# Attention, then two feed-forward layers, in one kernel on one core: a new plan for the first stage, a new weight conversion, and an addition by TensorE

## The chip, the cores and the metric

The kernel runs on one core of one Trainium2 chip. The metric is device time in microseconds (us) of one execution. The core has TensorE (matmul), VectorE, ScalarE, GpSimd and SyncE, which each run their own list of instructions in order and wait for one another by semaphores. SyncE issues nearly all DMA transfers.

## The reference

Three parts, in fp32 with inputs of the types that `setup_inputs()` gives:

- Attention over 4 batches, 8 heads, 576 positions, head size 64. Queries, keys and values are averaged over groups of 4 positions, full softmax attention runs on the 144 averages, and its output is repeated 4 times. To this is added a local attention in which a position sees only positions less than 4 away. So `x = out_up + out_local`, 2304 tokens by 512.
- First layer: `h = x @ w_in` (2048 columns), `g = s * relu(h)**2 + b`, `x = g @ w_out`.
- Second layer: `a = x @ w_a`, `c = x @ w_b` (1536 columns each), `out = (a * c) @ w_out`.

## The kernel before, in words

The matrices of the layers are multiplied with fp32 operands split in two parts, a high part in the faster fp32r type and the remainder as low part. Each product is three matmuls: high by high, high by low, low by high.

**Phase A** is the first layer. The tokens come in 6 blocks of 384. For each block, 16 steps f run over 128 columns of `w_in` each: four groups of three matmuls into the bank h (L1162 to L1164), ReLU (L1179) and square (L1183) on ScalarE, a copy that makes the high part (L1186, ScalarE), a subtraction for the low part (L1190, VectorE), and twelve matmuls into four banks acc (L1205 to L1207). **Phase B** is the second layer (L1269 on).

Before a block's products can start, its tokens must be there as high and low parts (xs). Blocks 0 and 1 get theirs from the **ramp**: six tiles of 128 tokens (`tile_job`, L802), which do the local attention on TensorE: scores (L843, L851), softmax on VectorE and ScalarE (L878 to L929), transposes (L937), products with the values (L956). VectorE adds the pooled output (L973) from upT, ScalarE makes the high part (L569), VectorE the low part (L573). Blocks 2 to 5 get theirs from 13 **band units** (`unit`, L988), which do the local attention on VectorE, some 17 us each; they start when the ramp has ended (L1664). For each batch, `down` (L630) does the pooled attention head pair by head pair: pooling of q and k (L654 on VectorE, L656 and L657 on GpSimd), scores (L688), softmax, transposes (L739), products with the pooled values (L760). For batches 1 to 3 the pooled values pv are made by transfers alone (`pool_in`, L611): a load by SyncE (L621) and three accumulating transfers by GpSimd for each half (L623), six in all, into one buffer.

**Weights** arrive as 64-bit floats, 512 KB a slice. A slice of phase A (32 of them, two for each f) is converted by `w_words` (L393) and `w_slice` (L439): ScalarE scales the high word into z (L414) and takes the low bits (L421), VectorE puts the sign in (L426) and joins both (L434), ScalarE copies the high part (L450), VectorE subtracts for the low part (L455).

**Order.** A planner in the kernel's Python code (`Program.order`, L168) simulates all engines with a fixed cost for each task and issues the task that can start first, ties by due time. Its list is the order of each engine's instructions on the chip. Due times hang on T0 (the wanted start of block 0) and the DUE constants (L71 to L76). Fill matmuls on zeros (`keep_warm`, L327) are put ahead of a task where the plan sees TensorE waiting, until block 0 has begun.

Of the kernel before, what the change touches and what calls it, by code (L numbers as in the profile page):

```python
# [17 lines left out]
HP = H // 2  # L18
# [5 lines left out]
TQ = 64  # L24
# [55 lines left out]
RAMP_BUFS = {"dq": 2, "dk": 2, "qd": 4, "kd": 4, "tq": 1, "tk": 1, "tv": 1, "e": 1, "x": 1, "z": 2}  # L80
# [7 lines left out]

ISSUE, QUEUE, DMA_START, POOL_START, DMA_LAND, POOL_NEXT = 0.46, 8, 1.29, 2.15, 1.18, 0.8
# [3 lines left out]
class Task:  # L93
    __slots__ = (
        "eng", "dur", "fn", "deps", "succ", "acq", "picks", "rel", "due", "lead", "share", "num", "left", "ready", "start",
        "end", "fill", "seen", "dma", "order", "wait",
# [3 lines left out]
class Clock:  # L100


    TICK, COLUMNS = 3.41333, 1.4

    def __init__(self):
        self.done = {}

    def run(self, start, work, share, keep=True):
        t = start
        while work > 1e-9:  # L110
            k = int(t / self.TICK + 1e-6)
            rate = 1.0 if self.done.get(k - 1, 0.0) >= self.COLUMNS else 0.5
            d = min(work / rate, (k + 1) * self.TICK - t)
            if keep:
                self.done[k] = self.done.get(k, 0.0) + d * rate * share
            work -= d * rate
            t += d
        return t
# [20 lines left out]
class Program:  # L139
# [8 lines left out]
    def add(self, eng, dur, fn, reads=(), writes=(), acq=(), rel=(), due=1e9, after=(), lead=0.0, share=1.0, seen=None, dma=(), order=0, wait=0.0):  # L148
# [5 lines left out]
        t.lead, t.share = lead, share  # L154
# [13 lines left out]
    def order(self):  # L168
# [9 lines left out]
        clock, warming, wire = Clock(), True, Wire()  # L178
        landed, adding = [], 0.0
        at["SP"] = 0.75  # L180
        at["PE"] = clock.run(1.07, 0.17 * WARM, 1.0)
# [9 lines left out]
        while len(out) < len(self.tasks):  # L191
            best = None
            for e in ENGINES:
                for t in avail[e]:
# [3 lines left out]
                    if e == "SP" and len(landed) >= QUEUE:  # L198
                        s = max(s, landed[-QUEUE])
# [34 lines left out]
            if t.eng == "PE":  # L234
                g0 = at["PE"]
# [41 lines left out]
def dve(n):  # L277
    return n / 960 + 0.065

# [10 lines left out]
def moe_chain(ctx, tc, qT, kT, vd, tq, tk, tv, qu, ku, vu, w_a1, w_o1, w_a2, w_b2, w_o2, sb, ident_d, bmask_d, emask_d, out):  # L290
# [30 lines left out]

    def bank(tag, shape, name):
        return ps.tile(shape, F32, tag=tag, name=name, bufs=4 if tag == "acc" else 2)

    pw = []

    def keep_warm(count):  # L327

        for _ in range(count):
            nc.tensor.matmul(out=pw[0], lhsT=wz[:, :128], rhs=wz, start=True, stop=True)  # L330

    def load(dst_src, nbytes, reads=(), writes=(), acq=(), rel=(), due=1e9, after=(), rows=128, pieces=1, base=0):
        def fn(picks):
            dst, src = dst_src(picks)
            nc.sync.dma_start(out=dst, in_=src)
# [35 lines left out]
    add("CTL", 0.0, warm_fn, acq=[("acc",)], due=-1e6)  # L371
# [21 lines left out]
    def w_words(k, spool, z, first, name, acq=(), after=()):  # L393
# [36 lines left out]
        add("DVE", 0.53, s_fn, [("low", k)], [("sg", k)], wait=PATIENCE)  # L430
# [5 lines left out]
        add("DVE", 0.6, b_fn, [("z", k), ("sg", k)], [name], rel=[ld_pick(ld), "stg"], wait=PATIENCE)  # L436
        return tz

    def w_slice(k, ph, lo_eng, after=()):  # L439
# [6 lines left out]
        w_words(k, ("w",), z, (), ("t", k), [(ph + "z",)], after)  # L446

        def h_fn(picks):
            wt[k] = slot(picks[0], F32R)
            A_.activation(out=wt[k][:, 0], in_=st["z"], func=ACTF.Copy)  # L450

        add("ACT", 0.52, h_fn, [("t", k)], [("wh", k)], [("w",)], wait=PATIENCE)
# [26 lines left out]
    def w_out(p, t, after, due=1e9):  # L479
# [8 lines left out]
        if t == 0:  # L488
# [8 lines left out]
            def s_fn(picks):  # L497
                nc.sync.dma_start(out=wod[p], in_=st["z"])
# [60 lines left out]
    def split_x(st, t0, n, xkey, ph, due):  # L559

        done = 0
        last = None
        while done < n:
# [4 lines left out]
            def hi(picks, i=i, o=o, w=w, done=done):  # L568
                A_.activation(out=xs["a", i][0][:, :, o:o + w], in_=st["x"][:, :, done:done + w], func=ACTF.Copy)  # L569

            def lo(picks, i=i, o=o, w=w, done=done):
# [6 lines left out]
            th = add("ACT", act(HP * w), hi, [xkey, ("slot", ("a", i))], [("xsh", i)], due=due)  # L578
            last = add(
                "DVE", dve(HP * w), lo, [xkey], [("xs", i)], due=due, after=[th] + ([last] if last else []),  # L580
                rel=[ph + "x"] if done + w == n else (),
# [29 lines left out]
    def pool_in(b, after, due):  # L611
# [3 lines left out]
        for r in range(4):  # L615
            for kh in range(2):
                def fn(p, r=r, kh=kh):
                    if r == kh == 0:
                        pooled[b] = upp.tile([HK, 2, HP, 2 * D], F32, tag="pv", name="pv", bufs=1)
                    if r == 0:  # L620
                        nc.sync.dma_start(out=pooled[b][:, kh], in_=src[:, kh, :, r])  # L621
# [5 lines left out]
                    [t[kh]] if r else [t[0]] if kh else after, order=kh if r == 0 else 0, seen=0.1, dma=[wires(HK, HP, 512, 0, r > 0)],  # L627
                )

    def down(b, hp, ph, pool_eng, due=1e9):  # L630
# [53 lines left out]
        def s_fn(p):  # L684
# [9 lines left out]
            "PE", 0.7, s_fn, [("qd", key), ("kd", key)], [("sc", key)], [wide, wide, E_SLOT[ph]],  # L694
            [ph + "qd", ph + "kd"], lead=LEAD, share=0.5)
# [48 lines left out]
        tt = add("PE", 0.52, t_fn, [("a", key), "ident"], [("at", key)], [wide, wide], lead=LEAD, share=0.5625)  # L744
# [10 lines left out]
        def o_fn(p):  # L755
# [46 lines left out]
    def tile_job(i, due):  # L802
# [35 lines left out]
        def s_fn(p):  # L838
# [22 lines left out]
            after=[mm["dS", bl, hp] for hp in range(HP)], lead=LEAD, share=0.55,  # L861
# [71 lines left out]
        def t_fn(p):  # L933
# [7 lines left out]
            lead=LEAD, share=0.75,  # L941
# [8 lines left out]

        def o_fn(p):
            o = st["o"] = bank(p[0], [128, HP, TT], "o")
            for hp in range(HP):
                for g in range(NQ):
                    for h in range(2):
# [3 lines left out]
                            rhs=st["aT"][:, h, hp, g * TQ:g * TQ + TQ], start=True, stop=True,  # L959
# [4 lines left out]
            "PE", 1.1, o_fn, [("taT", i), ("tv", i), ("slot", ("a", blk))] + [("up", b) for b in batches], [("to", i)], [WIDE],  # L964
            [pick(ts, 2), pick(t_v, 0)], lead=LEAD, share=0.8,
# [12 lines left out]

# [816 lines left out]
```

## Time and profile before

| | |
|---|---|
| median of 3 runs | 928.06 us (927.93, 928.06, 933.91) |
| profiled execution | 933.64 us, span 931.8 us |
| TensorE matmul busy | 909.6 us, 98% |
| VectorE busy | 781.5 us, 84% |
| ScalarE busy | 480.9 us, 52% |
| GpSimd busy | 72.4 us, 8% |

Times in the profile are us from the first instruction; the span ends with the last. A busy TensorE is not TensorE at its peak, since matmuls overlap in the records: a matmul of 384 columns shows 0.34 us and the next one starts 0.18 us later. In slices of 1/40 of the span, TensorE's granted clock is full but for the third (0.9) and the fourth (0.7).

### The profile page before, as it was taken

What the parts mean: (1) busy time and instruction counts of PE and PEld (TensorE: products, weight loads), DVE (VectorE), ACT (ScalarE), POOL (GpSimd) and SP (SyncE); (2) the same over time, 40 slices, a digit from 0 to 9 for tenths busy, and PEclk for the clock granted to TensorE, in tenths of its full rate; (3) what the DMA queues carried; (4) which work ended last, traced back from release to release, by engine and by line L of the source; (5) the groups of instructions that cost most, each with busy time, mean ns of one, the idle gap of its engine ahead of it and who ended that gap; (6) DMA issues with size and microseconds to landing.
All of it is one profiled execution on the core that took longest, in us unless ns stands there. A gap on an engine that the chain in (4) does not pass through costs nothing.

```text
span 931.8 us, 14461 instructions
## 1 busy us (share of the span) xinstructions
PE 909.6 (98%) x5456; PEld 847.6 (91%) x5456; DVE 781.5 (84%) x1383; ACT 480.9 (52%) x1017; POOL 72.4 (8%) x73
## 2 busy tenths in 40 slices
PE   8996999999999999999999999999999999999998
PEld 5685999999999899999999899998999999999997
DVE  7995898999999999995977999779877779877753
ACT  4694994335544454445987545336433336433322
POOL 0531122002222210000000000000000000000000
PEclk9997999999999999999999999999999999999999
DMA  9972936224345432314667232002200000200001
GB/s 244 273 258 62 289 89 206 82 69 128 105 118 116 133 89 69 102 29 161 213 228 256 93 107 75 23 23 102 86 23 26 26 11 35 102 23 24 1 1 68
DMA packets 47145, 97.07 MB, mean 104 GB/s; under 512 B 6396, under 2 KB 21884, under 8 KB 46692
## 3 DMA queue, kind: packets, MB, share of 16 engines
q1 hardware_dynamic: 39444, 93.09, 30.9%
q0 software_dynamic: 7200, 2.67, 2.4%
q8 instruction: 43, 0.70, 0.3%
q10 hardware_dynamic: 432, 0.39, 0.1%
q14 instruction: 26, 0.21, 0.1%
HBM read 83.54 MB, written 12.58 MB: 103 GB/s over the span
## 4 chain that ended last, share of the span: by engine, by line
PE 81%; DVE 8%; issue 5%; DMA 3%; POOL 2%; ACT 1%; SPq 0%; DVEq 0%; POOLq 0%; ACTq 0%
PE ab L1451 29%; PE acc L1205 6%; PE acc L1206 6%; PE acc L1207 6%; PE h L1162 6%; PE h L1163 5%; PE acc L1592 5%; PE h L1164 5%; PE acc L1593 5%; PE acc L1591 5%; DVE pr L1072 1%; PE o L760 1%; DMA x<-x2d 1%; DVE gl L1190 1%; DMA w<-in_qT_dram 1%
## 5 line engine op out<-in xcount | busy, mean ns | idle before, releaser
L1451 PE MATMUL ab<-xo,w 128*128 128x384 f32 x1332 | 270.2, 339 | 0.0
L1451 PEld LDWEIGHTS ab<-xo,w 128*128 128x128 f32 x1332 | 239.0, 188 | 16.0 <-DVE u L1525 1.7
L1205 PE MATMUL acc<-gh,w 128*128 128x384 f32 (+1 forms) x384 | 132.6, 345 | 1.0 <-ACT w L421 0.6
L1162 PE MATMUL h<-xsh,w 128*128 128x384 f32 x384 | 132.4, 345 | 0.0
L1206 PE MATMUL acc<-gl,w 128*128 128x384 f32 x384 | 130.1, 339 | 0.4 <-DVE gl L1190 0.4
L1207 PE MATMUL acc<-gh,w 128*128 128x384 f32 (+1 forms) x384 | 129.9, 338 | 0.0
L1163 PE MATMUL h<-xsl,w 128*128 128x384 f32 x384 | 129.8, 338 | 0.0
L1164 PE MATMUL h<-xsh,w 128*128 128x384 f32 x384 | 129.7, 338 | 0.0
L1179 ACT ACTIVATE u<-h 128x384 f32<-128x384 f32 x96 | 47.1, 491 | 124.3 <-PE h L1164 121.5
L1567 ACT ACTIVATE gh<-u 128x384 fp32r<-128x384 f32 x68 | 35.6, 524 | 86.7 <-DVE u L1528 50.2
L1205 PEld LDWEIGHTS acc<-gh,w 128*128 128x128 f32 x384 | 72.3, 188 | 4.5 <-issue 1.9
L1162 PEld LDWEIGHTS h<-xsh,w 128*128 128x128 f32 x384 | 72.6, 189 | 2.0 <-issue 1.8
L1206 PEld LDWEIGHTS acc<-gl,w 128*128 128x128 f32 x384 | 72.5, 189 | 0.9 <-DVE gl L1190 0.8
L1163 PEld LDWEIGHTS h<-xsl,w 128*128 128x128 f32 x384 | 72.8, 189 | 0.0
L1164 PEld LDWEIGHTS h<-xsh,w 128*128 128x128 f32 x384 | 72.6, 189 | 0.0
L1207 PEld LDWEIGHTS acc<-gh,w 128*128 128x128 f32 x384 | 72.5, 189 | 0.0
L1475 ACT ACTIVATE w<-ab 128x384 f32<-128x384 f32 x33 | 16.2, 491 | 100.6 <-PE ab L1451 100.5
L1190 DVE TENSOR_TENSOR gl<-u,gh 128x384 fp32r<-128x384 f32 x96 | 53.0, 552 | 11.5 <-ACT gh L1186 11.1
L1593 PE MATMUL acc<-wx,gl 128*128 128x512 f32 x141 | 55.6, 394 | 0.0
L1592 PE MATMUL acc<-wx,gh 128*128 128x512 f32 x141 | 55.4, 393 | 0.0
L1591 PE MATMUL acc<-wx,gh 128*128 128x512 f32 x141 | 55.4, 393 | 0.0
L426 DVE TENSOR_SCALAR w<-w 128x512 uint16<-128x512 f32 x59 | 42.5, 769 | 11.4 <-ACT w L421 11.4
(205 smaller groups left out, 1712.3 us busy)
## 6 DMA issues: line engine op xcount, KB each, us to landing
w<-in_w_o_dram SPq DMA_DIRECT2D x25, 512.0 KB
w<-in_w_a_dram SPq DMA_DIRECT2D x24, 512.0 KB
bk<-in_ku_dram SPq DMA_DIRECT2D x22, 320.0 KB
bk<-in_vu_dram SPq DMA_DIRECT2D x22, 320.0 KB
w<-wod SPq DMA_DIRECT2D x12, 512.0 KB
w<-in_w_b_dram SPq DMA_DIRECT2D x10, 512.0 KB
x2d<-ev SPq DMA_DIRECT2D x24, 192.0 KB
x<-x2d SPq DMA_DIRECT2D x3, 1536.0 KB
```

Of the source, the lines that this page charges most:

```text
L1162: nc.tensor.matmul(out=st["h"], lhsT=w[:, 0, k], rhs=hi[:, k], start=(k == 0), stop=False)
L1163: nc.tensor.matmul(out=st["h"], lhsT=w[:, 0, k], rhs=lo[:, k], start=False, stop=False)
L1164: nc.tensor.matmul(out=st["h"], lhsT=w[:, 1, k], rhs=hi[:, k], start=False, stop=(k == HP - 1))
L1179: A_.activation(out=st["u"], in_=st["h"], func=ACTF.Relu)
L1190: V.tensor_tensor(out=st["lo"], in0=st["u"], in1=st["hi"][:, :n].bitcast(F32), op=ALU.subtract)
L1205: nc.tensor.matmul(out=acc, lhsT=wh, rhs=st["hi"], start=(f == 0), stop=False)
L1206: nc.tensor.matmul(out=acc[:, :n], lhsT=wh, rhs=st["lo"], start=False, stop=False)
L1207: nc.tensor.matmul(out=acc, lhsT=wl, rhs=st["hi"], start=False, stop=(f == FA - 1))
L1451: nc.tensor.matmul(out=o, lhsT=w[:, k], rhs=x, start=(not more and k + n == 0), stop=(k == 1 and n == 2), skip_group_check=more,)
L1591: nc.tensor.matmul(out=acc, lhsT=gh, rhs=w[:, 0], start=first, stop=False)
L1592: nc.tensor.matmul(out=acc, lhsT=gh, rhs=w[:, 1], start=False, stop=False)
L1593: nc.tensor.matmul(out=acc, lhsT=gl, rhs=w[:, 0], start=False, stop=last)
```

## The change: what it does

Numbers in the kernel's code are in us.

1. **Conversion of phase A's weights.** VectorE takes the sign by a bitwise AND of z into a buffer of its own (sg, two of them), ScalarE writes the low bits into that buffer's low halves, VectorE joins both as before. The slot that the slice was loaded into is released after ScalarE's step. One in three high copies goes to VectorE (H_ENG), and so do the copies of block 0's squares (Q_ENG). z has three buffers instead of two.
2. **Addition by TensorE.** For tiles 0 to 2 an identity matmul puts the pooled output into the bank first and the products with the values are accumulated on it; the addition L973 goes, and L569 and L573 read the bank.
3. **The planner.** TensorE's clock is modelled anew, and so are the fetching of its instructions and the late landing of GpSimd's transfers (1.5 each, and the last seen 2.0 later instead of 0.1). Up to 20 fills may stand ahead of any ramp task of TensorE, and go into the bank that the task will use.
4. **Transfers.** Each of SyncE's first 96 transfers but the first 8 waits for the eighth before it.
5. **Constants.** T0, LEAD, the DUE times.

```diff
+UP_PE = 3
+H_ENG, XH_ENG, Q_ENG = "AAD", "A", "D"
-POOL_PREP = 2.0
-CONST_ENG, DUE_CONST = "G", 13.6
+POOL_PREP, VISIT = 2.0, 0.2
+CONST_ENG, DUE_CONST = "G", 12.3
-T0, STEP = 32.0, 4.018 / 384
-LEAD = 15.2
-DUE_DOWN = (7.3, 7.1, 8.6, 17.2)
-DUE_NEXT = (57.9, 0.8)
-DUE_TILE = (5.8, 19.7, 21.3)
-DUE_JOB = (12.0, 11.2, 13.0)
+T0, STEP = 27.6, 4.018 / 384
+LEAD = 14.1
+DUE_DOWN = (5.3, 4.5, 19.0, 1.7)
+DUE_NEXT = (62.2, 0.8)
+DUE_TILE = (7.9, 6.9, 0)
+DUE_JOB = (9.3, 12.6, 9.8)
-WARM, FILL_MIN, FILL_MAX = 18, 0, 20
+WARM, FILLS, FILL, FILL_COLUMNS, KEEP_COLUMNS = 18, 20, 0.172, 408, 2376.3
...
+POOL_LATE = 1.5
+RAMP_QUEUE, RAMP_LOADS, SP_WAIT = 8, 96, 0.15
...
-                if "acc" in t.rel:
-                    warming = False
-                while warming and t.fill < FILL_MAX and (t.fill < FILL_MIN or clock.run(g0, 0.17, 1.0, False) < s):
-                    g0 = clock.run(g0, 0.17, 1.0)
+                while t.fill < t.fills:
+                    end = clock.run(g0, FILL, FILL_COLUMNS, False)
+                    if end > s and clock.window(max(s, g0) + t.dur) + t.cols >= clock.KEEP:
+                        break
+                    g0 = fetch.run(clock, g0, FILL, FILL_COLUMNS, 2)
                     t.fill += 1
...
+    def send(out, in_):
+        made = nc.sync.dma_start(out=out, in_=in_)
+        ins = getattr(made, "ins", made)
+        if RAMP_QUEUE <= len(loads) < RAMP_LOADS:
+            tc.add_manual_dep(ins, loads[-RAMP_QUEUE].name, behind, reason="few transfers at once")
+        loads.append(ins)
...
+        def sw_fn(picks):
+            st["low"] = sg(picks)
+            V.tensor_scalar(
+                out=st["low"], in0=st["z"].bitcast(I32), scalar1=-(1 << 31), scalar2=None, op0=ALU.bitwise_and
+            )
+
+        def aw_fn(picks):
+            low_fn(st["low"].bitcast(U16).rearrange("p (m c) -> p m c", c=2)[:, :, 0])
...
+        if sg:
+            add("DVE", copies(DM), sw_fn, [("z", k)], [("sg", k)], [("rsg",)], wait=PATIENCE)
+            add("ACT", 0.56, aw_fn, [("st", k), ("sg", k)], [("low", k)], rel=done, wait=PATIENCE)
+        else:
+            add("ACT", 0.56, a_fn, [("st", k)], [("low", k)], wait=PATIENCE)
+            add("DVE", 0.53, s_fn, [("low", k)], [("sg", k)], wait=PATIENCE)
...
-                    [t[kh]] if r else [t[0]] if kh else after, order=kh if r == 0 else 0, seen=0.1, dma=[wires(HK, HP, 512, 0, r > 0)],
+                    [t[kh]] if r else [t[0]] if kh else after, order=kh if r == 0 else 0, seen=2.0 if r == 3 else 0.1, dma=[wires(HK, HP, 512, 0, r > 0)],
...
+            if up_pe:
+                for b in batches:
+                    gs = [g for g in range(NQ) if grp[g][0] == b]
+                    a, w, g0 = gs[0] * TQ, len(gs) * TQ, grp[gs[0]][1] // 4
+                    nc.tensor.matmul(
+                        out=o[:, :, a:a + w].rearrange("p h (g r) -> p h g r", r=4), lhsT=ident,
+                        rhs=upT[b][:, :, g0:g0 + w // 4].unsqueeze(3).to_broadcast([128, HP, w // 4, 4]), start=True, stop=True,
+                    )
...
-                            rhs=st["aT"][:, h, hp, g * TQ:g * TQ + TQ], start=True, stop=True,
+                            rhs=st["aT"][:, h, hp, g * TQ:g * TQ + TQ], start=not up_pe, stop=True,
+                            skip_group_check=up_pe,
...
+        eng = Q_ENG[f % len(Q_ENG)] if i == 0 else "A"
+
         def q2_fn(p):
-            A_.activation(out=st["hi"][:, :n], in_=st["u"], func=ACTF.Copy)
+            if eng == "D":
+                V.tensor_copy(out=st["hi"][:, :n], in_=st["u"])
+            else:
+                A_.activation(out=st["hi"][:, :n], in_=st["u"], func=ACTF.Copy)
```

## Rows read from the trace of the kernel before

**Rows 1.** Busy time by stage: start:end, us, each engine's busy us, clock, DMA share, GB/s.
```profile
47.20:75.80 28.60, 25.88 (x220) 23.88 (x218) 27.50 (x63) 27.36 (x70) 7.54 (x7) 0.94 0.74 237
75.80:94.00 18.20, 10.25 (x54) 8.30 (x54) 7.50 (x16) 5.90 (x13) 2.78 (x3) 0.62 0.24 45
94.00:147.00 53.00, 52.51 (x349) 50.81 (x348) 45.73 (x86) 48.35 (x96) 9.42 (x6) 1.00 0.67 196
147.00:214.00 67.00, 67.00 (x393) 66.45 (x392) 64.65 (x82) 28.64 (x57) 6.59 (x8) 1.00 0.33 104
```

**Rows 2.** Waits of TensorE, whole span: who, for whom, us in total, times, longest.
```profile
PE o L760 <- DMA pv<-in_vd_dram: 8.0, 2, 4.3
PE sc L688 <- POOL qd L657: 2.2, 1, 2.2
```

**Rows 3.** Timeline of TensorE: start, us, what, count, idle before.
```profile
84.54 0.75 PE L760 MATMUL o<-w,pv 72*64 72x144 f32 x4 [3.63 <-DMA pv<-in_vd_dram]
...
86.03 0.52 PE L1207 MATMUL acc<-gh,w 128*128 128x386 f32 x1
...
94.20 0.33 PE L1207 MATMUL acc<-gh,w 128*128 128x386 f32 x1
```

**Rows 4.** Timeline of GpSimd (POOL), 26 to 81 us.
```profile
26.36 0.45 POOL L657 TENSOR_TENSOR kd<-dk 128x144 f32<-128x144 f32 x1
...
32.00 1.33 POOL L623 DMA_DIRECT2D pv<-in_vd_dram  x1 [0.27 <-DMA pv<-in_vd_dram]
...
48.97 1.69 POOL L657 TENSOR_TENSOR qd<-dq 128x144 f32<-128x144 f32 x1
50.60 1.22 POOL L623 DMA_DIRECT2D pv<-in_vd_dram  x1
...
80.34 1.20 POOL L623 DMA_DIRECT2D pv<-in_vd_dram  x1 [3.27 <-issue]
```

**Rows 5.** Waits of SyncE's queue, 0 to 120 us.
```profile
SPq L621 <- DMA pv<-in_vd_dram: 22.5, 1, 22.5
```

**Rows 6.** Timeline of VectorE (DVE): the last split for block 2.
```profile
213.06 0.90 DVE L573 TENSOR_TENSOR xsl<-x,xsh 128x512 fp32r<-128x512 f32 x1
```

**Rows 7.** Timeline of TensorE: the first product of block 2.
```profile
214.29 0.34 PE L1162 MATMUL h<-xsh,w 128*128 128x384 f32 x1
```

**Rows 8.** VectorE's groups, 47.2 to 147 us (busy us, mean ns, idle before), then a wait.
```profile
L455 DVE TENSOR_TENSOR w<-z,w 128x512 fp32r<-128x512 f32 x30 | 20.9, 699 | 3.3 <-ACT w L450 3.2
L426 DVE TENSOR_SCALAR w<-w 128x512 uint16<-128x512 f32 x29 | 20.7, 775 | 7.7 <-ACT w L421 7.7
L1190 DVE TENSOR_TENSOR gl<-u,gh 128x384 fp32r<-128x384 f32 x16 | 8.9, 558 | 2.9 <-ACT gh L1186 2.9
...
DVE z L434 <- ACT z L414: 2.9, 4, 1.8
```

**Rows 9.** ScalarE's (ACT) groups, 47.2 to 147 us.
```profile
L450 ACT ACTIVATE w<-z 128x512 fp32r<-128x512 f32 x30 | 18.6, 625 | 0.0
...
L1186 ACT ACTIVATE gh<-u 128x384 fp32r<-128x384 f32 x17 | 8.9, 521 | 0.1
```

**Rows 10.** Timeline of VectorE: two sign steps and what starts after them.
```profile
102.32 1.36 DVE L426 TENSOR_SCALAR w<-w 128x512 uint16<-128x512 f32 x2
103.44 0.74 DVE L455 TENSOR_TENSOR w<-z,w 128x512 fp32r<-128x512 f32 x1
```

**Rows 11.** Line L573: ns minimum/median/maximum, and its shapes.
```profile
L573 DVE TENSOR_TENSOR xsl<-x,xsh x19: 414/683/898, 39.3 to 427.6; 128x512 fp32r<-128x512 f32 x17, 128x256 fp32r<-128x256 f32 x2
```

**Rows 12.** VectorE's groups, 23.7 to 47.2 us.
```profile
L973 DVE TENSOR_TENSOR x<-o,up 128x512 f32<-128x512 f32 x3 | 2.0, 677 | 0.0
```

**Rows 13.** TensorE's groups, 0 to 47.2 us: the fill matmuls.
```profile
L330 PE MATMUL pw<-wz 128*128 128x408 bf16 x112 | 23.6, 355 | 1.1 <-DVE ones L350 1.1
```

**Rows 14.** Timeline of TensorE: four products with the identity and the next matmul.
```profile
208.82 0.60 PE L1102 MATMUL bt<-ident,o 128*128 128x128 f32 x4
209.18 0.42 PE L1205 MATMUL acc<-gh,w 128*128 128x384 f32 x1
```

More of the change, by code (lines that the diff above doesn't have):

```diff
@@ L94 @@
     __slots__ = (
-        "eng", "dur", "fn", "deps", "succ", "acq", "picks", "rel", "due", "lead", "share", "num", "left", "ready", "start",
-        "end", "fill", "seen", "dma", "order", "wait",
+        "eng", "dur", "fn", "deps", "succ", "acq", "picks", "rel", "due", "lead", "cols", "fills", "num", "left", "ready", "start",
+        "end", "fill", "seen", "words", "dma", "order", "wait",
     )
 class Clock:
-    TICK, COLUMNS = 3.41333, 1.4
-    def __init__(self):
-        self.done = {}
@@ L108, in run @@
[L108 to L117, printed above, removed]
+    TICK, FIRST, COLUMNS, KEEP, FULL = 3.41333, 3360.0, 2600.0, KEEP_COLUMNS, 2400.0
@@ L146, in __init__, with add @@
         self.free = {k: [0.0] * n for k, n in free.items()}
-    def add(self, eng, dur, fn, reads=(), writes=(), acq=(), rel=(), due=1e9, after=(), lead=0.0, share=1.0, seen=None, dma=(), order=0, wait=0.0):
+    def add(self, eng, dur, fn, reads=(), writes=(), acq=(), rel=(), due=1e9, after=(), lead=0.0, cols=0.0, fills=0, words=12, seen=None, dma=(), order=0, wait=0.0):
         t = Task()
@@ L320, in new @@
         return pools[ph].tile(shape, dtype, tag=tag, name=tag, bufs=n_bufs[ph][tag])
-    def bank(tag, shape, name):
[L323 to L330, printed above, removed]
+    todo = [0]
+    loads = []
+    behind = mybir.DependencyInfo(mybir.DependencyClass.Sync, mybir.DependencyReason.DATA)
+    def send(out, in_):
[4 more added lines that the diff above has]
+        loads.append(ins)
+    def bank(tag, shape, name):
+        whole = ps.tile([128, 512], F32, tag=tag, name=name, bufs=4 if tag == "acc" else 2)
+        for _ in range(todo[0]):
+            nc.tensor.matmul(out=whole[:, :408], lhsT=wz[:, :128], rhs=wz, start=True, stop=True)
+        todo[0] = 0
+        n = 1
+        for k in shape[1:]:
+            n *= k
+        part = whole[:shape[0], :n]
+        if len(shape) == 3:
+            part = part.rearrange("p (a b) -> p a b", b=shape[2])
+        if len(shape) == 4:
+            part = part.rearrange("p (a b c) -> p a b c", b=shape[2], c=shape[3])
+        return part
     def load(dst_src, nbytes, reads=(), writes=(), acq=(), rel=(), due=1e9, after=(), rows=128, pieces=1, base=0):
@@ L444, in z, with sg @@
             return st["z"]
-        w_words(k, ("w",), z, (), ("t", k), [(ph + "z",)], after)
+        def sg(picks):
+            return new(ph, "sg", [128, DM], I32)
+        w_words(k, ("w",), z, (), ("t", k), [(ph + "z",)], after, sg)
+        eng = H_ENG[k % len(H_ENG)]
         def h_fn(picks):
             wt[k] = slot(picks[0], F32R)
-            A_.activation(out=wt[k][:, 0], in_=st["z"], func=ACTF.Copy)
-        add("ACT", 0.52, h_fn, [("t", k)], [("wh", k)], [("w",)], wait=PATIENCE)
+            if eng == "D":
+                V.tensor_copy(out=wt[k][:, 0], in_=st["z"])
+            else:
+                A_.activation(out=wt[k][:, 0], in_=st["z"], func=ACTF.Copy)
+        name, cost = ("DVE", copies(DM)) if eng == "D" else ("ACT", 0.52)
+        add(name, cost, h_fn, [("t", k)], [("wh", k)], [("w",)], wait=PATIENCE)
         def l_fn(picks):
@@ L557, in moe_chain, with split_x @@
         xs_slot(key, blocks_of[key])
-    def split_x(st, t0, n, xkey, ph, due):
+    def split_x(st, t0, n, xkey, ph, due, held=None, made=None):
         done = 0
         last = None
+        eng = XH_ENG if ph == "r" and not held else "A"
         while done < n:
@@ L576, in lo @@
                 )
[L578 removed]
+            name, cost = ("DVE", copies) if eng == "D" else ("ACT", act)
+            if held:
+                cost = lambda n: act(n, True)
+            th = add(name, cost(HP * w), hi, [xkey, ("slot", ("a", i))], [("xsh", i)], due=due)
             last = add(
                 "DVE", dve(HP * w), lo, [xkey], [("xs", i)], due=due, after=[th] + ([last] if last else []),
[L581 removed]
+                rel=[held or ph + "x"] if done + w == n else (),
             )
@@ L860, in tile_job @@
             [("tsc", i)], [WIDE, WIDE, ("re", "w")], () if kept else ["rtq", "rtk"],
-            after=[mm["dS", bl, hp] for hp in range(HP)], lead=LEAD, share=0.55,
+            after=[mm["dS", bl, hp] for hp in range(HP)], lead=LEAD, cols=1400, fills=FILLS if ph == "r" else 0, words=32 * NQ + 4 * (1 if len(set(variant)) == 1 else NQ),
         )
```

154 lines of the change are left out of this document (118 added, 36 removed).

## The prediction

> **What bounds the kernel now.** I read the busy times by stage first [rows 1]. From the first product of block 0 at 47.2 us to the end of that block at about 147 us TensorE is the engine to watch; before 47.2 us it mostly fills time, after 147 us it is never short of work for long. Of these 99.8 us, 18.2 (75.8 to 94.0) hold 10.25 us of TensorE work at a mean clock of 0.62. The waits name the cause [rows 2]: 8.0 us for the pooled values of batch 1 (pv), and 2.2 us for a pooling step of GpSimd. The timeline shows the second loss [rows 3]: a matmul of 384 columns takes 0.52 us at 86.0 us and 0.33 us at 94.2 us, so after the wait TensorE runs at the lower of its two levels (1.2 of 2.4 GHz).
>
> Why pv is late stands on GpSimd [rows 4]. Its six accumulating transfers of batch 1 go one by one: the first is issued at 32.0 us, the second at 50.6 us, behind GpSimd's own pooling steps, the last at 80.3 us; the products that read pv end their wait at 84.5 us. SyncE suffers from the same buffer: its load for batch 2 needs pv free and holds the queue for 22.5 us [rows 5], so no weights come in meanwhile, and VectorE works 7.50 of the 18.2 us.
>
> Then I looked for what would stop TensorE if these waits went. VectorE ends the last split for block 2 at 213.06 + 0.90 us [rows 6], and block 2's first product starts at 214.29 us [rows 7]. There is no slack: from 147 to 214 us VectorE is busy 64.65 of 67 us [rows 1]. It must finish the weight conversions of phase A before the band units, and the units before block 2. **So the time is set by how much sooner VectorE is through, and TensorE's 8.0 us are no measure of the gain.** TensorE can follow, for its own losses are larger: 8.0 and 2.2 us of waits, and half of the about 9 us from 84.5 to 94.
>
> **The change part by part.** The sum is made against the profiled execution, 933.64 us with a span of 931.8 us and 1.8 us around it. It lies 5.6 us above the median of 928.06 us; two of the three runs are near 928, the third at 933.91. What these 5.6 us are, one trace cannot tell. I correct nothing for it and put it on the low end of the range.
>
> *Plan of the pooled values.* The new planner adds 1.5 us to each accumulating transfer and makes the last ones visible 1.9 us later, so six in a row lie 6 x 1.5 + 1.9 = 10.9 us later in the plan than by the old count, more than the 8.0 us that the products came too early. TensorE then has other matmuls ahead of them, and SyncE's load for batch 2 stands behind more weight loads. Batch 1's due time also moves from 32.0 + 64.3 - 57.9 = 38.4 to 27.6 + 64.3 - 62.2 = 29.7 us by the constants of the code. I give back all VectorE idleness of that stretch: 18.2 - 7.5 = 10.7 us. What is late next is VectorE itself.
>
> *ScalarE.* From 94 to 147 us it is busy 48.35 of 53 us [rows 1], and VectorE is idle 53 - 45.73 = 7.3 us. A third of the high copies (10 of 32) and block 0's 16 copies of the square leave it: 10 x 0.62 + 16 x 0.52 = 14.5 us [rows 9] of busy time. I take 6.3 of the 7.3 us back. In the stretch before, VectorE is idle 28.6 - 27.5 = 1.1 us [rows 1]; I take 1.0.
>
> *VectorE's new work.* The sign step L426 is replaced for 32 slices by a bitwise AND over whole rows, and the 10 + 16 copies arrive. No row shows such an operation. Upper end: L426 itself, two in 103.44 - 102.32 = 1.12 us, 0.56 each [rows 10]. Lower end: what 256 elements less save, 0.683 - 0.414 = 0.27 us [rows 11], so 0.29. I take 0.40, a little nearer the lower end, because L426 reads every second word and writes every fourth half-word while the new ones touch whole rows; 384 columns cost three quarters, 0.30. So: 32 x (0.40 - 0.56) = -5.1; 10 x 0.40 = +4.0; 16 x 0.30 = +4.8. The three additions that go to TensorE save three operations in 2.0 us, 1.9 of pace [rows 12]. Together +1.8 us.
>
> The Trainium skill, "VectorE: DVE Perf Modes", section "The perf-mode tier table", gives fp32 copies and tensor_scalar in SBUF twice the pace of a two-source operation. L426 has one source in SBUF and takes 775 ns at the mean, no less than the 699 ns of the two-source L455 [rows 8], so the trace does not bear this out yet; by the rule the sum would be 6.5 us lower (a rival, below).
>
> *Identity matmul.* 512 columns. Lower end: four 128-column products with the identity, 209.18 - 208.82 = 0.36 us [rows 14]. Upper end: four products of 144 columns in 0.75 us at the lower clock [rows 3], which for 512 columns run singly is 0.67 us. I take 0.6, 1.8 us for three tiles. Cost on the path: nothing, since TensorE spends 23.6 us before 47.2 us on fill matmuls [rows 13]; without that cover 1.8 us. The bank is held until the low part is written, some 1.3 us longer; block 0's accumulators are not open then.
>
> *Fills.* Now possible ahead of each of the ramp's tasks, also after block 0 has begun. The plan places them where TensorE would idle: nothing, at worst as many again as the 94 behind the first 18 of now, 94 x 23.6 / 112 = 20 us [rows 13].
>
> *Loads.* Each SyncE transfer among the first 96 waits for the eighth before it. Behind it stand all later loads, and ScalarE's conversions wait for those. With eight of 512 KB in flight the wire stays busy: nothing, 2 us where the eight are small. The order by new due times, the earlier constants and the third z buffer change only who is served first: nothing, plus or minus 3 us.
>
> **Sum:** 10.7 + 6.3 + 1.0 - 1.8 = 16.2 us, 933.6 - 16.2 = 917.4 us.
>
> **The rivals.**
> *Double pace (911 us).* If the new operations run at half of 0.56 us, they cost 32 x -0.28 + 10 x 0.28 + 16 x 0.21 - 1.9 = -4.7 us, and the gain is 18.0 + 4.7 = 22.7 us. For it: one source and whole rows. Against it: L426's own pace.
> *No pace gained (926 us).* All at 0.56 and 0.42 us: 5.6 + 6.7 - 1.9 = +10.4, gain 7.6 us. The change then does not do on VectorE what the plan says.
> *pv stays late (928 us).* Without the 10.7 us the gain is 5.5 us. For it: GpSimd already slows when VectorE is full; its 144-column step takes 0.45 us at 26.4 us and 1.69 us at 49.0 us [rows 4], and the accumulations stay one behind the other. The Trainium skill, "SBUF — State Buffer", section "SBUF: two separate sides", says that one-source VectorE copies lock GpSimd out of a shared port and so delay the descriptors of its transfers. The slowed step agrees with a lock, and the change adds such copies; no run here shows the delay on a transfer. Against it: the 10.9 us more that the plan allows.
> *Slower (941 us).* A slice now passes ScalarE and VectorE in turn six times (z, sign, low, join, high, low part), where the two first steps of ScalarE stood together before. Both engines work in order, so one late hand-over stops both. VectorE's waits for z are 2.9 us in 4 [rows 8], 0.73 each; one such wait for each of 32 slices is 23.4 us, 917.4 + 23.4 = 940.8. It turns the gain into a loss from 16.2 / 32 = 0.51 us a slice. Against it: three z buffers in place of two, so that three slices can be under way.
>
> **How the numbers follow.** Forecast 0.42, double pace 0.25, pv late 0.15, no pace gained 0.10, slower 0.08. A measurement tells about 1% from no change: faster is below 918.8 us, slower above 937.3. The forecast lies close to that edge, and the 5.6 us pull it down, so two thirds of it count as faster: 0.28 + 0.24 of double pace + 0.05 of the others = 0.57. Slower is 0.08, the rest 0.35. Range: up to pv late with 1 us for the loads, 929; down to double pace less the 5.6 us and 1 us, 904. The slower case and about 0.1 of tails stay outside.
>
> **What would show it.** Right: no wait for pv over 2 us, TensorE at full clock from block 0 to the end of phase A, SyncE not held by the batch 2 load, the last conversion 12 to 20 us earlier, block 2's first product again just behind its last split, by about 16 us sooner. The AND at 0.3 to 0.45 us. Wrong: a new wait of VectorE for ScalarE's low or z step on most slices; a pv wait elsewhere; TensorE idle before block 2 although block 0 ended early, which would mean that VectorE's work, not the stall, was the price.

## The result and the profile after

The changed kernel takes 919.42 us (median of 5 runs, 918.99 to 925.97), the kernel before 928.06 us (5 runs beside them, 926.42 to 933.91): ratio 0.9905 [0.9876, 0.9933]. Measured again (e0 below) the ratio was 0.9933 [0.9909, 0.9957]. The profiled execution is the longest of the five, 925.97 us with a span of 923.9 us at a mean granted clock of 0.992; the other four lie between 918.99 and 919.63 us at 0.997 to 1.000.

TensorE's waits over the whole span (who, for whom, us in total, times, longest) answer to [rows 2]: the wait for pv is 3.4 us in place of 8.0, the one for GpSimd's qd is gone.

```profile
PE o L881 <- DMA pv<-in_vd_dram: 3.4, 1, 3.4
```

Busy times by stage answer to [rows 1] (start:end, length; PE, PEld, DVE, ACT, POOL busy; clock, DMA share, GB/s). Block 0 now runs from 44.8 to 138 us, 93.2 us long in place of 99.8.

```profile
44.80:83.00 38.20, 37.98 (x312) 36.24 (x311) 38.02 (x93) 36.58 (x82) 3.77 (x3) 1.00 0.92 293
83.00:100.50 17.50, 14.15 (x64) 11.58 (x63) 10.13 (x25) 7.15 (x16) 2.39 (x2) 0.61 0.26 69
100.50:138.00 37.50, 37.44 (x269) 36.40 (x268) 30.56 (x68) 27.67 (x51) 5.98 (x5) 1.00 0.59 149
138.00:205.30 67.30, 67.27 (x391) 65.74 (x389) 65.11 (x83) 29.05 (x57) 6.02 (x8) 1.00 0.34 106
```

TensorE's timeline answers to [rows 3] (start, us, what, count, idle before). After the 3.35 us of idleness the matmuls run at the lower level again, 0.52 us each and 0.32 apart, until 100 us.

```profile
87.34 0.75 PE L881 MATMUL o<-w,pv 72*64 72x144 f32 x4 [3.35 <-DMA pv<-in_vd_dram]
...
91.88 0.52 PE L1352 MATMUL acc<-gl,w 128*128 128x384 f32 x1
...
100.27 0.34 PE L1303 MATMUL h<-xsh,w 128*128 128x384 f32 x1
```

GpSimd's timeline answers to [rows 4]. The accumulating transfers are no earlier: the last is issued at 83.14 us in place of 80.34, and pv is there 4.2 us after it, as before.

```profile
39.79 2.07 POOL L778 TENSOR_TENSOR qd<-dq 128x144 f32<-128x144 f32 x1
41.79 1.65 POOL L744 DMA_DIRECT2D pv<-in_vd_dram  x1
...
83.14 1.20 POOL L744 DMA_DIRECT2D pv<-in_vd_dram  x1 [5.19 <-issue]
```

Groups of VectorE and ScalarE in block 0 answer to [rows 8, 9] (line, what, count, busy us, mean ns, idle before). L523 is the new AND, L561 and L1328 the copies that came to VectorE, L510 ScalarE's low step into sg.

```profile
L569 DVE TENSOR_TENSOR w<-z,w 128x512 fp32r<-128x512 f32 x30 | 20.1, 685 | 4.4 <-ACT w L563 4.4
L540 DVE SCALAR_TENSOR_TENSOR z<-z,sg 128x512 int32<-128x512 int32 x29 | 19.5, 687 | 5.7 <-ACT sg L510 5.6
L523 DVE TENSOR_SCALAR sg<-z 128x512 int32<-128x512 int32 x28 | 11.6, 424 | 0.5 <-ACT z L505 0.5
...
L1328 DVE CAST gh<-u 128x384 fp32r<-128x384 f32 x16 | 5.8, 363 | 1.5 <-ACT u L1322 1.5
L561 DVE CAST w<-z 128x512 fp32r<-128x512 f32 x9 | 3.8, 421 | 0.0
...
L510 ACT ACTIVATE sg<-w 128x512 uint16<-128x512 uint16 x28 | 21.8, 796 | 0.1
L563 ACT ACTIVATE w<-z 128x512 fp32r<-128x512 f32 x20 | 12.6, 638 | 2.3 <-DVE z L540 2.3
```

VectorE's timeline answers to [rows 10]: an AND and a copy of 512 columns start 0.34 us before what follows them.

```profile
126.96 0.42 DVE L561 CAST w<-z 128x512 fp32r<-128x512 f32 x1
127.30 0.42 DVE L523 TENSOR_SCALAR sg<-z 128x512 int32<-128x512 int32 x1
127.64 0.68 DVE L569 TENSOR_TENSOR w<-z,w 128x512 fp32r<-128x512 f32 x1
```

Block 2's first product with a low part still stands right behind its last split [rows 6, 7], 8.8 us sooner: the split ends at 204.31 + 0.85 us.

```profile
204.31 0.85 DVE L691 TENSOR_TENSOR xsl<-x,xsh 128x512 fp32r<-128x512 f32 x1
...
205.22 0.44 PE L1302 MATMUL h<-xsl,w 128*128 128x384 f32 x1
```

### The profile page after: what moved, and what is told of

Its sections match the earlier page's. It is cut to its first block, busy times and chain, and to the rows that moved or that the text cites. A ratio compares the mean times of both kernels' runs of the same rounds, so it can differ in the third digit from the quotient of the medians.

```text
span 923.9 us, 14427 instructions
## 1 busy us (share of the span) xinstructions
PE 908.5 (98%) x5437; PEld 844.3 (91%) x5437; DVE 777.6 (84%) x1406; ACT 471.9 (51%) x991; POOL 68.1 (7%) x73
## 4 chain that ended last, share of the span: by engine, by line
PE 77%; DVE 13%; issue 6%; DMA 1%; POOL 1%; ACT 0%; SPq 0%; DVEq 0%; POOLq 0%
PE ab L1597 29%; PE acc L1738 5%; PE acc L1739 5%; PE acc L1737 5%; PE acc L1351 5%; PE acc L1352 5%; PE h L1301 5%; PE acc L1353 5%; PE h L1302 5%; PE h L1303 5%; DVE pr L1150 2%; DVE pr L1211 2%; DVE s L1156 1%; DVE gl L1334 1%; DVE nb L823 1%
## 5 line engine op out<-in xcount | busy, mean ns | idle before, releaser
L1597 PE MATMUL ab<-xo,w 128*128 128x384 f32 x1318 | 266.2, 338 | 0.0
L1597 PEld LDWEIGHTS ab<-xo,w 128*128 128x128 f32 x1318 | 235.7, 188 | 16.1 <-DVE u L1671 1.5
L1621 ACT ACTIVATE w<-ab 128x384 f32<-128x384 f32 x33 | 16.2, 491 | 100.3 <-PE ab L1597 100.3
L1739 PE MATMUL acc<-wx,gl 128*128 128x512 f32 x156 | 61.5, 394 | 0.0
L1738 PE MATMUL acc<-wx,gh 128*128 128x512 f32 x156 | 61.4, 393 | 0.0
L1737 PE MATMUL acc<-wx,gh 128*128 128x512 f32 x156 | 61.3, 393 | 0.0
L1150 DVE TENSOR_TENSOR pr<-bq,bk 128x1792 f32<-128x1792 f32 (+1 forms) x26 | 49.5, 1903 | 2.7 <-DMA bq<-in_qu_dram 2.3
```

Of the source, the lines that this page charges most:

```text
L1150: V.tensor_tensor(out=pr, in0=st["q", h].unsqueeze(2).to_broadcast([128, R, 7, D]), in1=window(st["k", h], R), op=ALU.mult,)
L1597: nc.tensor.matmul(out=o, lhsT=w[:, k], rhs=x, start=(not more and k + n == 0), stop=(k == 1 and n == 2), skip_group_check=more,)
L1737: nc.tensor.matmul(out=acc, lhsT=gh, rhs=w[:, 0], start=first, stop=False)
L1738: nc.tensor.matmul(out=acc, lhsT=gh, rhs=w[:, 1], start=False, stop=False)
L1739: nc.tensor.matmul(out=acc, lhsT=gl, rhs=w[:, 0], start=False, stop=last)
```

## The experiments

The theory from the prediction: TensorE's wait for pv makes VectorE idle, the length of block 0 is set by VectorE's idleness in it, and the conversion takes more idleness away. Rivals: the conversion or the new order is what gains; or the idleness would go without any gain.

First a look at how a wait of TensorE reaches VectorE, which the prediction left to SyncE's queue. ScalarE's and VectorE's timelines of the kernel before, around the wait:

```profile
85.34 0.29 ACT L772 ACTIVATE up<-o 128x144 f32<-128x144 f32 x1 [8.57 <-PE o L760]
85.53 0.67 ACT L421 ACTIVATE w<-w 128x512 int32<-128x512 uint16 x1
...
78.06 0.74 DVE L434 SCALAR_TENSOR_TENSOR z<-z,w 128x512 int32<-128x512 int32 x1
86.23 0.75 DVE L426 TENSOR_SCALAR w<-w 128x512 uint16<-128x512 f32 x1 [7.43 <-ACT w L421]
```

ScalarE stands 8.57 us at L772, the copy of the pooled output `up`, since TensorE is late with it. Behind it in ScalarE's list stands the low step L421, and VectorE's next instruction, the sign step L426, needs that: 7.43 us. No load stands in this chain.

### e6, e4: take the late transfers away

The accumulating transfers of batch 1 are left out, so pv holds one of its four addends; the plan still has them. e6 does it to the kernel before, e4 to the changed one.

```diff
-                    else:
+                    elif b > 1:
                         G.dma_start(out=pooled[b][:, kh], in_=src[:, kh, :, r], accum_op=ALU.add)
```

> The kernel before without the six accumulating transfers of batch 1 (pooled values left incomplete), order unchanged. It prices the late pooled values in the old plan. If the 10.7 us of idle VectorE are what they cost: 9 to 13 us less than the kernel before, so that nearly the whole gain of the change is there. Rival (something else holds block 0 as long): 0 to 4 us less.

> The changed kernel without the six accumulating transfers of batch 1 (its pooled values are left incomplete); order and all other work unchanged. The 3.4 us wait of TensorE for pv goes, and with it the stretch at half clock where a run has one. V: 918 to 920 us, since VectorE's work is the same. T: 916 us or less, 3.4 us from the wait alone.

Measured: e6 918.75 us, ratio 0.9892 [0.9868, 0.9916]; e4 918.97 us, 0.9887 [0.9867, 0.9907]. Neither has a wait for pv nor a stretch at the lower clock. Stages of e6:

```profile
47.20:75.80 28.60, 26.63 (x237) 23.55 (x237) 28.60 (x65) 28.57 (x71) 0.00 (x0) 1.00 0.53 204
75.80:94.00 18.20, 17.91 (x172) 16.49 (x167) 17.18 (x36) 17.72 (x38) 2.55 (x2) 1.00 0.86 294
94.00:132.10 38.10, 37.86 (x214) 37.17 (x213) 33.26 (x62) 33.59 (x67) 6.88 (x4) 1.00 0.54 142
```

Without the wait the kernel before is about 10 us faster (0.0108 x 928.78) and level with the changed one. So the wait is worth all that the change gained; the rest of the change comes to nothing in sum. (Without the transfers GpSimd and the DMA engines also have less to do; e8, below, keeps them.)

### e8, e9: the planner's count of these transfers alone

e8 puts two numbers of the change into the kernel before: 1.5 us more for each accumulating transfer in the plan, and the last one of a half seen 2.0 us after its landing in place of 0.1. e9 takes the same two out of the changed kernel.

```diff
+                if t.eng != "SP":
+                    done += 1.5
...
-  ... order=kh if r == 0 else 0, seen=0.1, ...
+  ... order=kh if r == 0 else 0, seen=2.0 if r == 3 else 0.1, ...
```

> The kernel before with one part of the change alone: the plan counts each accumulating transfer of GpSimd 1.5 us later and the last of a half visible 2.0 us later. Theory P (the later count of these transfers is what moves the wait for pv, and that is the gain): the wait for pv falls from 8.0 us to under 4, block 2 is ready at 203 to 207 us in place of 214, and the time is 918 to 923 us. Theory Q (the count alone moves little; the new order by due times or the conversion is what counts): wait for pv over 6 us, 925 to 930 us.

> The changed kernel with that part undone: no 1.5 us for each accumulating transfer, no 1.9 us for the last. Theory P: the products with pv come too early again, a wait for pv of 6 us or more, 925 to 929 us. Theory Q: the wait stays under 4 us and the time within 2 us of the changed kernel, 918 to 921 us.

Measured: e8 919.08 us, ratio 0.9889 [0.9868, 0.9911]. e9 926.11 us, 0.9962 [0.9939, 0.9984]. e8's TensorE reaches the products with pv at 86.70 us, behind a run of block 0's matmuls and without idleness, and its stages have full clock:

```profile
86.43 0.34 PE L1209 MATMUL acc<-gh,w 128*128 128x386 f32 x1
86.70 1.20 PE L762 MATMUL o<-w,pv 72*64 72x144 f32 x16
...
47.20:75.80 28.60, 27.19 (x267) 23.46 (x265) 28.47 (x68) 28.09 (x80) 7.36 (x5) 1.00 0.86 281
75.80:94.00 18.20, 18.07 (x150) 16.85 (x149) 17.85 (x36) 18.20 (x40) 2.30 (x2) 1.00 0.28 65
94.00:135.60 41.60, 40.96 (x256) 39.97 (x255) 36.62 (x69) 36.96 (x74) 6.92 (x6) 1.00 0.72 212
```

e9 comes to them too early again, and ScalarE's copy of `up` is again what holds the others:

```profile
76.64 0.47 PE L881 MATMUL o<-w,pv 72*64 72x144 f32 x4 [2.32 <-DMA pv<-in_vd_dram]
80.70 1.71 PE L881 MATMUL o<-w,pv 72*64 72x144 f32 x12 [3.60 <-DMA pv<-in_vd_dram]
...
81.50 0.29 ACT L893 ACTIVATE up<-o 128x144 f32<-128x144 f32 x1 [6.55 <-PE o L881]
```

Two numbers give the whole gain; without them the change keeps 0.0038 of its 0.0067 to 0.0095, though e9's interval overlaps e0's [0.9909, 0.9957]. e8 also shows what SyncE's queue was worth. Before its load for batch 2 the queue waits 23.0 us, 15.5 for pv and 7.5 for the products that read it; in the kernel before it is 28.5 us, 22.5 [rows 5] and 6.0 (e8's line numbers are two higher):

```profile
SPq L623 <- DMA pv<-in_vd_dram: 15.5, 1, 15.5
SPq L623 <- PE o L762: 7.5, 1, 7.5
...
SPq L621 <- PE o L760: 6.0, 1, 6.0
```

In e8 VectorE works 17.85 of the 18.2 us from 75.8 us on all the same.

### e10, e11: the conversion without the wait

Both are e4 (transfers of batch 1 left out). e11 has all copies of high parts on ScalarE and keeps the AND; e10 has the old conversion as well.

```diff
-H_ENG, XH_ENG, Q_ENG = "AAD", "A", "D"
+H_ENG, XH_ENG, Q_ENG = "A", "A", "A"
...
-        w_words(k, ("w",), z, (), ("t", k), [(ph + "z",)], after, sg)
+        w_words(k, ("w",), z, (), ("t", k), [(ph + "z",)], after)
```

> The changed kernel without batch 1's accumulating transfers (left out of the computation, so that no wait for pv disturbs) and with the old conversion: the sign step on every second word, ScalarE's two first steps together, all copies on ScalarE. Beside it stands the same kernel with the new conversion (918.97 us). Theory C (the conversion is worth what the sum gave it, 6.3 us of ScalarE relief less 1.8 to 3 of VectorE): 922 to 926 us. Theory N (the conversion is worth nothing, as block 0 is limited by three engines at once): 917.5 to 920.5 us.

> The changed kernel without batch 1's accumulating transfers and with all copies of high parts back on ScalarE, the AND kept. ScalarE gets back about 9 x 0.63 + 16 x 0.52 = 14 us of work in block 0, VectorE loses 9 x 0.42 + 16 x 0.36 = 9.5 us busy. Theory C (ScalarE's load is what stops block 0): 923 to 930 us. Theory N: 917 to 921 us. If VectorE alone sets the pace: 912 to 916 us.

Measured: e10 923.08 us, 0.9933 [0.9911, 0.9956]; e11 922.02 us, 0.9925 [0.9900, 0.9951]; against e4's 0.9887 (another set of runs of the kernel before). e10 is where theory C had it, e11 between the two theories. Inside the new plan the conversion is worth about 4 us (0.0046 x 929), by the medians 3.5 of it through the copies, though e11's interval touches e4's [0.9867, 0.9907]. This is the price of the conversion together with the order that the planner then makes, and in e10 it does not go the way of the theory, through VectorE to block 2. The first product of block 2 comes as early in e10 as in e4 (e11's comes at 199.9 us):

```profile
197.01 0.44 PE L1301 MATMUL h<-xsh,w 128*128 128x384 f32 x1
...
196.81 0.34 PE L1301 MATMUL h<-xsh,w 128*128 128x384 f32 x1
```

What e10's profiled run loses to e4's (spans 919.2 and 917.1 us) it loses on TensorE: up to the end of phase A it has about a dozen matmuls more to do from there (1758 records against 1745), some 2 us of work. Whether ScalarE's relief in block 0 makes that or the new order, is not shown.

The kernel before has the old conversion, and without the wait it is as fast as e4. So something else in the change costs what the conversion gives. The profiles show where. From the first product of block 2 to the end of phase A the same number of matmuls takes 292.4 us in e4 and 289.4 in e6:

```profile
196.81:489.20 292.39, 290.04 (x1745) 279.75 (x1745) 259.30 (x401) 162.89 (x375) 33.13 (x30) 1.00 0.41 130
...
199.69:489.10 289.41, 288.46 (x1745) 279.66 (x1745) 260.38 (x400) 162.94 (x375) 31.19 (x30) 1.00 0.42 131
```

The whole kernels show the same: 289.7 us before, 292.3 after and 292.4 in e0. What costs it, is not settled: a new cost reorders everything, and due times, constants, the fills, the addition by TensorE and the limit on loads were not tried one by one.

### e1, e2, e3: which engine limits block 0

The changed kernel with more work in block 0's steps on one engine, unknown to the plan: e1 runs the low-part subtraction twice (VectorE), e2 the ReLU twice (ScalarE), e3 the first matmul of each step four times (TensorE).

```diff
+            for _ in range(2 if i == 0 else 1):
                 V.tensor_tensor(out=st["lo"], in0=st["u"], in1=st["hi"][:, :n].bitcast(F32), op=ALU.subtract)
...
+            for _ in range(2 if i == 0 else 1):
                 A_.activation(out=st["u"], in_=st["h"], func=ACTF.Relu)
...
+                    for _ in range(3 if i == 0 and k == 0 else 0):
+                        nc.tensor.matmul(out=st["h"], lhsT=w[:, 0, k], rhs=hi[:, k], start=True, stop=True)
```

> The changed kernel with the low-part subtraction of block 0 done twice (the second writes the same values): 16 x about 0.47 = 7.5 us more of VectorE between 53 and 133 us, same order of everything else. Theory V (VectorE's total work up to block 2 sets the time): 925 to 927 us against 919.4 of the changed kernel, block 2's first product 6 to 8 us later. Rival T (TensorE's own time sets it, VectorE has room): 919 to 921 us.

> The changed kernel with block 0's ReLU done twice (same values): 16 x about 0.40 = 6.4 us more of ScalarE in block 0. V and T both: 919 to 921 us. Rival S (ScalarE sets the pace in block 0): 925 to 926 us.

> The changed kernel with the first matmul of each of block 0's 16 steps issued four times (same result): 48 x 0.175 = 8.4 us more of TensorE in block 0. V: 919 to 922 us, the added time is made up before block 2. T: 927 to 928 us.

Measured: e1 924.92 us, 0.9949 [0.9931, 0.9967]; e2 924.62 us, 0.9946 [0.9930, 0.9962]; e3 926.14 us, 0.9961 [0.9943, 0.9978]. Against the changed kernel's two ratios these are 1.5 to 4.1, 1.2 to 3.8 and 2.6 to 5.2 us for additions of 7.5, 6.4 and 8.4 us. Block 2 is ready 5.0, 1.9 and 5.0 us later than in e0 (203.7, 200.6, 203.7 against 198.7 us). No engine passes its addition on in full, and in the profiled runs none passes nothing on; the intervals of all three overlap e0's [0.9909, 0.9957]. e1 lies just short of what V had forecast, e2 of S and e3 of T, and the kernel before took 930.0 us beside them, not 928.06, so each falls further short than it looks. VectorE does not set the pace of block 0 alone, and neither does ScalarE or TensorE. From 44.8 us to the end of block 0 in e1 and in e3, one row of each:

```profile
44.80:136.30 91.50, 87.00 (x658) 79.84 (x657) 88.44 (x205) 73.34 (x152) 13.57 (x12) 1.00 0.68 200
```

```profile
44.80:136.20 91.40, 91.40 (x693) 88.10 (x694) 80.60 (x187) 72.60 (x150) 13.10 (x11) 1.00 0.69 202
```

### e5: work for VectorE after block 0

One large product of the first three band units runs twice, 5.8 us in all.

```diff
+                for _ in range(2 if u < 3 and h == 0 else 1):
                     V.tensor_tensor(
                         out=pr, in0=st["q", h].unsqueeze(2).to_broadcast([128, R, 7, D]), in1=window(st["k", h], R),
...
```

> The changed kernel with one of the four large products of VectorE done twice in each of the first three band units (same values): 3 x 1.93 = 5.8 us more of VectorE between block 0's end and block 2's start. Theory V (after block 0 VectorE's units set the time): 5 to 6 us more than the changed kernel in this call, all of it at block 2's first product. Rival T (TensorE's own time sets it): 0 to 1 us more.

Measured: 927.26 us, 0.9992 [0.9969, 1.0016], 5.5 us over e0's ratio. TensorE has a new wait for VectorE:

```profile
PE acc L1353 <- DVE gl L1335: 4.0, 4, 2.4
```

Here VectorE passes on nearly all it gets. The first product of block 2 comes at 203.1 us in place of e0's 198.5, so 4.5 of the 5.5 us are there by then; 2.0 of them already at the end of block 0, since the first of the doubled products runs there (128.5 to 132.6 us). From the band units to the start of block 2 VectorE sets the pace.

### e7 and e0: pv first, and the changed kernel again

e7 gives batch 1's transfers a due time 25 us earlier; e0 is the changed kernel itself.

```diff
-    pool_in(1, P.made["open", "r"], target(FA) - DUE_NEXT[0])
+    pool_in(1, P.made["open", "r"], target(FA) - DUE_NEXT[0] - 25)
```

> The changed kernel with batch 1's pooled values due 25 us earlier in the plan, so that GpSimd issues the accumulating transfers ahead of its own pooling steps. Theory P (what is left of the wait for pv is GpSimd's late second transfer): TensorE's wait of 3.4 us gone, 1 to 3 us less than the changed kernel. Rival (the earlier transfers push out loads that are needed first, or the plan comes out another way): the same or up to 5 us more.

> The changed kernel itself, on the chip and in the call of the three below. 0.990 of the kernel before. In most executions no stretch at half clock, then block 0 ends some 6 to 7 us sooner than in the profile shown.

Measured: e7 923.77 us, 0.9949 [0.9930, 0.9968]; e0 921.08 us (919.67 to 927.25), 0.9933. In e7 the products run at 77.7 us without a wait for pv, but the third tile is split only at 48.2 us (45.6 in e0), and TensorE has other waits:

```profile
PE sc L411 <- DVE xsl L691: 2.8, 1, 2.8
```

So earlier transfers gain nothing in this plan. That they take the queue from loads that the ramp needs would fit (SyncE issues pv's loads at 5.9 us in place of 20.8) but is not shown, since the planner ordered everything anew. e0's profiled execution (span 918.6 us) shows the same program with a wait for pv of 0.5 us and no stretch at the lower clock:

```profile
86.54 0.47 PE L881 MATMUL o<-w,pv 72*64 72x144 f32 x4 [0.50 <-DMA pv<-in_vd_dram]
...
46.40:83.00 36.60, 36.20 (x304) 34.21 (x301) 36.34 (x88) 34.82 (x80) 4.92 (x4) 1.00 0.90 289
83.00:100.50 17.50, 17.00 (x138) 15.08 (x138) 16.51 (x40) 14.95 (x31) 1.19 (x1) 1.00 0.60 167
100.50:131.10 30.60, 30.52 (x210) 29.78 (x205) 26.37 (x59) 21.84 (x40) 5.99 (x5) 1.00 0.56 133
```

## Why the prediction was right, point by point

The forecast of 917.4 us lies 2.0 below the median of 919.42. VectorE's busy time and idleness in block 0, summed from the stage rows, tell which terms carried it:

| kernel | block 0, us | VectorE busy | idle | block 2 ready at |
|---|---|---|---|---|
| before [rows 1] | 99.8 | 80.7 | 19.1 | 214.0 |
| after, profiled | 93.2 | 78.7 | 14.5 | 205.2 |
| after again (e0) | 84.7 | 79.2 | 5.5 | 198.7 |
| before, no late pv (e6) | 84.9 | 79.0 | 5.9 | 199.4 |
| before, new count (e8), from 47.2 | 88.4 | 82.9 | 5.5 | 202.9 |

(e8's block 0 begins at 50.5 us; part of its 82.9 us is still the ramp's.) VectorE's work hardly differs, so a shorter block 0 has less of its idleness; which of the two makes the other, the table cannot tell.

**The bound: right behind block 0, not shown inside it.** Block 2 is ready 67.1 to 67.6 us after the first copy out of block 0's banks in each of these five, and 70.1 us after it in e5, where VectorE has more to do; in e7, e10 and e11, whose orders the planner made anew, it is 64.0 to 64.5 us. Inside block 0 the stall stops VectorE and TensorE alike, and both accounts fit: from before to e6 VectorE's idleness falls by 13.2 us, TensorE's waits for pv (8.0) and what it loses at the lower clock (half of the 9 us behind them) come to 12.5, and block 0 is 14.9 us shorter. e1 and e3 do not part them either: 7.5 us more for VectorE and 8.4 us more for TensorE both put block 2 off by 5.0. So the 8.0 us alone were no measure of the gain, as the prediction said; that VectorE alone sets the pace in block 0 is not shown.

**The pv term, 10.7 us: right for the medians, too small for the profiled run, its way half wrong.** e8 gives 10.3 us (0.0111 x 929.51) and e6 10.0; from the profiled run of before to that of e6 the span falls by 14.7 us (931.8 to 917.1). The step that the products come later in the plan holds: TensorE comes to them at 83.5 us, where the kernel before came to them at 75.8, 4.32 us before this row:

```profile
80.16 0.75 PE L760 MATMUL o<-w,pv 72*64 72x144 f32 x4 [4.32 <-DMA pv<-in_vd_dram]
```

The step "so no weights come in meanwhile" falls as the reason of VectorE's idleness: in e8 the queue waits 23.0 us and VectorE idles 0.35 us. The wait went through ScalarE's copy of `up`, at the head of its list, and so to VectorE.

**The ScalarE terms, 6.3 and 1.0 us: wrong.** This is the step that failed, "I take 6.3 of the 7.3 us back". From 94 us to the end of block 0 VectorE is idle 7.3 us before, 4.8 in e6 and 5.0 in e8, both with the old conversion; the 1.1 us ahead of 75.8 us are 0.0 and 0.1 there. So a third of that idleness, and the 1.0, went with pv and not with ScalarE. (Per us it hardly changed, 7.3 in 53.0 against 4.8 in 38.1: with no stall less work was left for this stretch.) The rest stays in e0 too (30.60 - 26.37 = 4.2 us from 100.5 us on), although ScalarE's busy time in block 0 fell from 81.6 to 71.6 us. In the new plan e11 prices the copies on ScalarE at some 3.5 us, with its new order; beside the old plan, e6, nothing of it is left.

**VectorE's work, +1.8 us: better than forecast.** The AND and the copy start 0.34 us before what follows, against my 0.40, and a copy of 384 columns 0.27 (93.67 to 93.94 us; forecast 0.30). By my own count that is 32 x (0.34 - 0.56) + 10 x 0.34 + 16 x 0.27 - 1.9 = -1.2 us. The Trainium skill, "VectorE: DVE Perf Modes", section "The perf-mode tier table", gives fp32 copies in SBUF twice the pace of a two-source operation. The trace comes near it: 0.34 us against 0.60 (126.36 to 126.96 us, the subtraction L569), 1.8 times. The rival "double pace" had the price nearly right (0.28) and the time wrong: its 911 us stood on the ScalarE terms too. ScalarE paid for the AND: its low step takes 796 ns (L510), 673 before (L421).

**Near by luck, in part: two errors of opposite sign.** The forecast started 5.6 us above the median and took off 7.6 us more than the medians moved (16.2 against 8.6); what is left is the 2.0 us. The sum of 16.2 us stood against the profiled 933.64. From that run's span to e0's, 931.8 to 918.6, it is 13.2; the medians moved by 8.6. The pv term was 4 us too small for that run, and ScalarE's terms, of which nothing shows beside the old plan, were 7.3 too high. The 5.6 us between that run and the median, which I left in, may be a matter of the wait's length in one execution. The kernel before has one trace, so this is not shown for it; the changed kernel has 3.4 us of the wait in its profiled run and 0.5 in e0, with some 13 us at the lower clock or none, and 5.3 us of span between the two.

**Identity matmul, fills, loads: no cost seen, none tried alone.** The identity matmuls show as two records a tile and cost 1.02 to 1.13 us a tile, above both ends of the estimate (0.36 and 0.67). Two of the three tiles stand among the fills, of which 87 are left in place of 112 [rows 13]; the third, at 40.0 us, stands behind the last fill (38.1 us). With the limit on loads the DMA share is 0.92 from 44.8 to 83.0 us.

**The rivals.** "pv stays late" came half true: the last transfer is issued 2.8 us later than before. "Slower" fell: VectorE's join waits for ScalarE's new step in 3 cases of 29, 5.6 us in all in the profiled run and 0.6 us in e0, which has no such stall.

**The signs.** In e0 most of the signs named for "right" came: a wait for pv of 0.5 us, full clock, the last conversion 15.9 us earlier (it starts at 123.5 us, 139.4 before), block 2 ready 15.3 us sooner, the AND at 0.34 us. The profiled run of the result had a wait of 3.4 us, the lower clock, and a conversion 9.4 us earlier. "SyncE not held" came in neither: before batch 2's load the queue issues nothing from 78.7 to 95.9 us, in e0 from 80.8 to 91.3.

**What stays open.** e4 has block 2 ready 2.4 us before e6 (197.0 and 199.4 us) and both end with a span of 917.1. The 2.4 us are lost again by the end of phase A (292.4 against 289.4 us, above). TensorE's waits there explain 1.1 us (2.0 against 0.9); the rest is not accounted for.

## What to carry to other kernels

When a change has many parts and one wait stands out in the profile, put the part that touches that wait alone into the old kernel first: here two numbers of a plan gave all of it. Follow a wait through each in-order engine, for the instruction at the head of the list (here a small copy of ScalarE) decides who stops. Idleness behind a stall can go with the stall, here 2.4 of 7.3 us: try that before you book it under another term. And where one stall stops two engines, a fall in the idleness of one does not show that this one set the pace.

## What the runs showed of the hardware

The time from one accumulating transfer of GpSimd to the next lies between 4.1 and 12.6 us in these traces. Windows from issue to issue, of the changed kernel, of e8, of e0 and of the kernel before:

```profile
53.10:65.10 12.00, 12.00 (x95) 11.67 (x94) 11.82 (x29) 11.50 (x23) 1.24 (x2) 1.00 1.03 341
...
110.10:115.60 5.50, 5.50 (x37) 5.44 (x35) 5.50 (x15) 3.59 (x7) 1.23 (x2) 1.00 0.56 143
115.60:119.90 4.30, 4.30 (x51) 3.98 (x50) 3.36 (x7) 4.06 (x8) 1.22 (x2) 1.00 0.29 34
```

```profile
58.70:70.20 11.50, 11.34 (x98) 10.41 (x97) 11.50 (x26) 11.04 (x24) 2.04 (x2) 1.00 1.06 381
...
94.29:100.59 6.30, 6.30 (x67) 5.99 (x65) 5.96 (x14) 5.90 (x12) 1.19 (x1) 1.00 1.03 315
...
65.88:75.70 9.82, 9.27 (x53) 8.79 (x51) 9.82 (x22) 9.79 (x20) 1.20 (x2) 1.00 0.74 258
```

In the changed kernel's and e8's windows a long time goes with a high DMA share: 11.3 to 12.0 us at 0.91 to 1.06, 4.3 to 5.5 us at 0.29 to 0.56. As a rule it does not hold: e0 has 6.3 us at 1.03, and the kernel before 9.8 us at 0.74. The cause is open. The prediction had weighed the lock of the Trainium skill, "SBUF — State Buffer", section "SBUF: two separate sides". For GpSimd's pooling step the trace leaves room for it (2.07 us at 39.79 us). For the transfers it speaks against it: two ANDs stand in the 5.5 us from 110.1 and in the 4.3 us from 115.6, six in the 12.0 us from 53.1, about as densely, and e8, without the AND, has an interval of 11.5 us too. Fewer loads in flight while pv is made would be one trial.

A wait of TensorE of 3.35 us in block 0 was followed by 13 us at 1.2 GHz (a mean granted clock of 0.61 from 83.0 to 100.5 us), one of 0.50 us by none (1.00, the rows of the changed kernel and of e0 above).
